# Second MoE's weights: earlier loads, decoding in 13 of 16 units, and g's low part on VectorE

## The chip, the cores and the metric

The kernel runs on one core of one Trainium2 chip. The metric is the device time of one execution in microseconds (us). A run of the profiler on that core gives the trace from which the rows below are taken. Engines are named as in the profile: PE (TensorE matmuls), PEld (its weight loads), DVE (VectorE), ACT (ScalarE), POOL (GpSimd) and SP, whose queue issues all the DMAs.

## What is computed

Three stages follow one another: a complex-decay attention (4 batches, 8 heads, 768 steps, head size 48), an MoE with a mish-like gate (384 to 2048 to 384), and a bilinear MoE (384 to 1536 to 384), on 3072 tokens.

```python
# attention: per step, S = a * S + k v^T (complex decay a, normalised), y = q . Re(S)
x = y.transpose(0, 2, 1, 3).reshape(3072, 384)
h = x @ w_in                                 # first MoE
g = h * tanh(log1p(exp(min(h, 20))))
x = g @ w_out
a, b = x @ w_a, x @ w_b                      # second MoE
out = (a * b) @ w_out2
```

All five weight matrices arrive as 64-bit floats, q, k, v and the decay as 32-bit floats.

## The kernel before

**Tiles and units.** The tokens are cut into 6 blocks of 512 (128 steps of each batch). The first MoE goes through a block in 16 units f: 9 matmuls of `moe1_h` make one 128 x 512 tile of h, `mish_factor` and `mish_product` turn it into g, and two units later (`lag`) 9 matmuls of `moe1_x2` add g times w_out into three PSUM tiles. Every product is made of three matmuls on split operands (high x high, high x low, low x high), so each weight and each activation has a high part, rounded, and a low part, the rest. `mish_product` makes them for g: `gh` on ACT in blocks 0 and 5 (`on_act`) and on DVE otherwise (L511 to L514), `gl` by one subtraction on POOL (L515). The second MoE has 12 units in each of its 6 blocks: 9 + 9 matmuls for a and b, then 12 for the output.

**Attention beside it.** The attention of block j + 1 is spread over the units of block j, in slots. Block 0 has the most beside it: the attention of block 1 and the rest of the first MoE's own weights. Block 5 has no attention left, and in its place the second MoE's weights are prepared.

**Weights.** `load_weights` handles a piece of a 64-bit matrix, 128 x 768 elements, in three steps: a DMA on SP's queue into a staging tile `wraw`; `decode`, three DVE instructions on integer words (L150 to L152) that make a 32-bit float in a tile `wf32`; and `split`, the high part on ACT and the low part on POOL (L157). `pipeline(steps, 2)` yields once a call; a call splits one piece, decodes another and starts the load of a third. The first MoE has 16 pieces, the second 18 (a, b and o for six values of j).

**Where the second MoE's pieces stand.** At the first unit of block 5 `prepare` closes the attention's pools (`att.close()`) and opens two in their place: `w2a` for the pieces of j below `EARLY` = 2, and `st2a`, with two buffers for `wf32`, for staging. The other pieces take buffers of the first MoE's weights as these are used up. Every unit of block 5 makes one call of the pipeline, and the second MoE's units make the rest. The staging pool `wst` of the first MoE's weights belongs to the attention's pools; it has two `wraw` and one `wf32`.

**Order.** Waits and order on each engine are set by the tile framework when the kernel is built: it takes the program's order as a priority and moves an instruction ahead where its model says that its inputs and buffers are there. So the order on an engine is not that of the code. Each engine goes through its own list in order: an instruction that waits holds up what stands behind it.

Of the kernel before, what the change touches and what calls it, by code (L numbers as in the profile page):

```python
# [10 lines left out]
F32 = mybir.dt.float32  # L11
F32R = mybir.dt.float32r
# [9 lines left out]
def kernel(  # L22
# [97 lines left out]
    ps_h = w1.enter_context(tc.tile_pool(name="ps_h", bufs=2, space=PSUM))  # L120
    ps_x = w1.enter_context(tc.tile_pool(name="ps_x", bufs=1, space=PSUM))

    att = right.enter_context(ExitStack())
    ap1 = att.enter_context(tc.tile_pool(name="ap1", bufs=1, side="right"))
    ap2 = att.enter_context(tc.tile_pool(name="ap2", bufs=2, side="right"))
    wst = att.enter_context(tc.tile_pool(name="wst", bufs=1, side="right"))
    am = [ap1.tile([P, HH, C], F32, name=f"am{i}") for i in range(2)]
    qT = [ap1.tile([P, HH, C], F32, name=f"qT{i}") for i in range(2)]
    W = [ap1.tile([P, H * D + PAD], F32, name=f"W{b}") for b in range(B)]
# [3 lines left out]
    def load_weights(nm, j, src, pool, place):  # L133


        a, b = src.shape[1:]
        if src.dtype == F32:
            raw = pool.tile([P, a, b], F32, tag="wraw", name="wraw", bufs=2)
            nc.sync.dma_start(out=raw, in_=src)
        else:  # L140
            b //= 2
            raw = pool.tile([P, a, b, 2], U32, tag="wraw", name="wraw", bufs=2)
            nc.sync.dma_start(out=raw.rearrange("p a b t -> p a (b t)"), in_=src)
        f = [raw]

        def decode():
            if src.dtype != F32:
                f[0] = pool.tile([P, a, b], F32, tag="wf32", name="wf32")
                fu, low, high = f[0].bitcast(U32), raw[..., 0], raw[..., 1]
                nc.vector.tensor_scalar(fu, high, 3, 0x3FFFFFFF, ALU.logical_shift_left, ALU.bitwise_and)  # L150
                nc.vector.scalar_tensor_tensor(fu, high, 0xC0000000, fu, ALU.bitwise_and, ALU.bitwise_or)  # L151
                nc.vector.scalar_tensor_tensor(fu, low, 29, fu, ALU.logical_shift_right, ALU.bitwise_or)  # L152

        def split():
            hi, lo = weights[nm, j] = [place(f"w{nm}{i}{j}", [P, a, b]) for i in "hl"]
            act(out=hi, in_=f[0], func=AF.Copy)
# [349 lines left out]
    def mish_product(p, m, on_act):  # L506

        nc.vector.scalar_tensor_tensor(m, m, 2.5, p, ALU.subtract, ALU.mult)  # L508
        gh = mp.tile([P, TN], F32R, tag="gh", name="gh")
        gl = mp.tile([P, TN], F32R, tag="gl", name="gl")  # L510
        if on_act:  # L511
            act(out=gh, in_=m, func=AF.Copy)
        else:
            nc.vector.tensor_copy(gh, m)  # L514
        nc.gpsimd.tensor_tensor(gl, m, gh.bitcast(F32), ALU.subtract)  # L515
        return gh, gl

    x2ps = {}
# [21 lines left out]

    x2h, x2l = {}, {}

    def load_w2(pool, early):


        for j in range(NF2 // 2):
            def place(name, shape, j=j):
                return early.tile(shape, F32R, name=name) if j < EARLY else shared(name, shape)

            for nm, src in (("a", wcols(w2_a, j)), ("b", wcols(w2_b, j)), ("o", wrow(w2_out, j))):  # L550
                yield lambda nm=nm, j=j, src=src, place=place: load_weights(nm, j, src, pool, place)

    def load_x2(b, pool):

        xh = x2h[b] = xp.tile([P, KM, TN], F32R, tag="xh", name="xh2")
        xl = x2l[b] = xp.tile([P, KM, TN], F32R, tag="xl", name="xl2")

        def step(t):
            raw = pool.tile([P, KM, C], F32, tag="xr", name="xr", bufs=2)
            nc.sync.dma_start(out=raw, in_=x2_d[b][:, t:t + C].rearrange("(k p) t -> p k t", p=P))  # L560

            def split():
                s = slice(t, t + C)
# [140 lines left out]
    mp = w1.enter_context(tc.tile_pool(name="mp", bufs=3))  # L704

    EARLY = 2

    def prepare():

        att.close()  # L710
        early = right.enter_context(tc.tile_pool(name="w2a", bufs=1, side="right"))
        spool = right.enter_context(tc.tile_pool(name="st2a", bufs=2, side="right"))
        steps = list(load_w2(spool, early))
        steps[3 * EARLY:3 * EARLY] = load_x2(0, spool)
        prep_pool.append(spool)
        yield from pipeline(steps, 2)

    prep_pool = []
    units = [(b, f) for b in range(NB) for f in range(NF)]
    ready, lag = {}, 2  # L720
    prep = None
    for ui in range(len(units) + lag):
        if ui < len(units):
            blk, f = units[ui]
            if f == 0:
                base = slot[0]
                want = ends[blk + 1] if blk + 1 < NB else n_slots
                if slot[0] == n_slots:
                    prep = prepare()
            p = moe1_h(blk, f, ps_a if prep and f % 2 else ps_h)  # L730
            do_w()
            run_to(base + (want - base) * (2 * f + 1) // (2 * NF))
            m = mish_factor(p)
            if prep:
                next(prep, None)
        if ui >= lag:
            moe1_x2(*units[ui - lag], *ready.pop(ui - lag))
        if ui < len(units):
            run_to(base + (want - base) * (2 * f + 2) // (2 * NF))
            ready[ui] = mish_product(p, m, blk in (0, NB - 1))  # L740

    w1.close()
    spool = prep_pool[0]
    p2 = allp.enter_context(tc.tile_pool(name="p2", bufs=3))
    one = allp.enter_context(tc.tile_pool(name="one", bufs=1))
    ps_o = allp.enter_context(tc.tile_pool(name="ps_o", bufs=1, space=PSUM))
# [208 lines left out]
```

## Time and profile before

| what | value |
|---|---|
| median of three runs (lowest to highest) | 1170.1 us (1168.77 to 1170.27) |
| the profiled execution's own time | 1166.57 us |
| its span, first to last instruction | 1164.9 us |
| PE busy | 1074.6 us (92%) |
| DVE busy | 711.3 us (61%) |
| ACT busy | 632.1 us (54%) |
| POOL busy | 350.1 us (30%) |
| granted TensorE clock, mean | 0.975 |

A row of a timeline is an instruction with its start and its duration, and in brackets how long its engine sat idle before it and what ended that. A row of windows gives, for a stretch of time, its length, how long PE, PEld, DVE, ACT and POOL were busy in it and with how many instructions, then the granted clock (1.00 is full speed), the DMA share and GB/s. DVE and POOL durations include time in which the instruction stands still for whatever reason, so the same form can have very different durations; the minimum is what it takes undisturbed.

### The profile page before, as it was taken

What the parts mean: (1) busy time and instruction counts of PE and PEld (TensorE: products, weight loads), DVE (VectorE), ACT (ScalarE), POOL (GpSimd) and SP (SyncE); (2) the same over time, 40 slices, a digit from 0 to 9 for tenths busy, and PEclk for the clock granted to TensorE, in tenths of its full rate; (3) what the DMA queues carried; (4) which work ended last, traced back from release to release, by engine and by line L of the source; (5) the groups of instructions that cost most, each with busy time, mean ns of one, the idle gap of its engine ahead of it and who ended that gap; (6) DMA issues with size and microseconds to landing.
All of it is one profiled execution on the core that took longest, in us unless ns stands there. A gap on an engine that the chain in (4) does not pass through costs nothing.

```text
span 1164.9 us, 15523 instructions
## 1 busy us (share of the span) xinstructions
PE 1074.6 (92%) x5788; PEld 904.7 (78%) x5788; DVE 711.3 (61%) x1062; ACT 632.1 (54%) x1050; POOL 350.1 (30%) x314
## 2 busy tenths in 40 slices
PE   2978887999999999999997788999999999999997
PEld 1856666888788878878875566888888888888886
DVE  5777989777777777778658998556242232322221
ACT  7767877878787877878756663212121221221221
POOL 6254665544444444444325663000000000000000
PEclk9988899999999999999998989999999999999999
DMA  7634553322233332223025444324010010100000
GB/s 132 139 104 116 136 153 66 90 49 48 56 82 68 64 75 49 48 55 82 22 82 163 138 134 148 102 87 151 1 55 1 9 47 1 34 7 1 28 1 29
DMA packets 187226, 83.01 MB, mean 71 GB/s; under 512 B 143821, under 2 KB 171530, under 8 KB 187146
## 3 DMA queue, kind: packets, MB, share of 16 engines
q1 hardware_dynamic: 187146, 81.97, 27.8%
q8 instruction: 47, 0.77, 0.3%
q14 instruction: 33, 0.27, 0.1%
HBM read 68.51 MB, written 13.43 MB: 70 GB/s over the span
## 4 chain that ended last, share of the span: by engine, by line
PE 46%; DVE 7%; ACT 2%; issue 1%; POOL 1%; DMA 1%; DVEq 0%; POOLq 0%; ACTq 0%; SPq 0%
PE ops L604 13%; PE psb L579 13%; PE psa L579 12%; PE hps L493 3%; PE x2ps L527 3%; DVE wf L151 2%; DVE wf L150 1%; ACT m L48 1%; DVE m L508 1%; DVE m L499 1%; PE py L372 1%; DVE wf L152 1%; POOL gl L515 1%; PE psc L348 1%; DMA wraw<-in_moe_w_a_dram 0%
## 5 line engine op out<-in xcount | busy, mean ns | idle before, releaser
L515 POOL TENSOR_TENSOR gl<-m,gh 128x512 fp32r<-128x512 f32 x96 | 136.3, 1419 | 130.8 <-DVE gh L514 99.4
L590 DVE TENSOR_TENSOR a_sb<-a_sb,psb 128x512 f32<-128x512 f32 x72 | 49.3, 685 | 198.2 <-PE psb L579 198.1
L48 ACT ACTIVATE m<-m 128x512 f32<-128x512 f32 x192 | 119.9, 627 | 70.8 <-DVE m L499 69.0
L48 ACT ACTIVATE ph<-a_sb 128x512 fp32r<-128x512 f32 x72 | 45.5, 632 | 179.4 <-DVE a_sb L590 179.4
L527 PE MATMUL x2ps<-gl,wouth 128*128 128x512 f32 x288 | 117.1, 407 | 20.2 <-POOL gl L515 20.2
L493 PE MATMUL hps<-xh,winh 128*128 128x512 f32 x288 | 122.5, 425 | 8.6 <-DVE xh L433 3.0
L48 ACT ACTIVATE a_sb<-psa 128x512 f32<-128x512 f32 x72 | 42.8, 596 | 159.0 <-PE psa L579 158.1
L493 PE MATMUL hps<-xl,winh 128*128 128x512 f32 x288 | 118.6, 412 | 4.6 <-DVE xl L434 4.6
L527 PE MATMUL x2ps<-gh,wouth 128*128 128x512 f32 x288 | 118.7, 416 | 2.8 <-ACT gh L48 2.8
L493 PE MATMUL hps<-xh,winl 128*128 128x512 f32 x288 | 117.4, 408 | 2.3 <-POOL winl L157 2.3
L527 PE MATMUL x2ps<-gh,woutl 128*128 128x512 f32 x288 | 115.5, 401 | 0.0
L508 DVE SCALAR_TENSOR_TENSOR m<-m,hps 128x512 f32<-128x512 f32 x96 | 65.4, 681 | 54.8 <-ACT m L48 54.7
L604 PE MATMUL ops<-woh,ph 128*128 128x384 f32 x288 | 97.2, 337 | 0.0
L604 PE MATMUL ops<-woh,pl 128*128 128x384 f32 x288 | 97.2, 337 | 0.0
L604 PE MATMUL ops<-wol,ph 128*128 128x384 f32 x288 | 96.8, 336 | 0.0
L579 PE MATMUL psb<-xh,wbh 128*128 128x512 f32 x216 | 84.7, 392 | 0.7 <-ACT a_sb L48 0.7
L579 PE MATMUL psa<-xh,wal 128*128 128x512 f32 x216 | 85.3, 395 | 0.0
L579 PE MATMUL psa<-xl,wah 128*128 128x512 f32 x216 | 85.3, 395 | 0.0
L579 PE MATMUL psa<-xh,wah 128*128 128x512 f32 x216 | 84.7, 392 | 0.0
L579 PE MATMUL psb<-xh,wbl 128*128 128x512 f32 x216 | 84.4, 391 | 0.0
L579 PE MATMUL psb<-xl,wbh 128*128 128x512 f32 x216 | 84.3, 390 | 0.0
L527 PEld LDWEIGHTS x2ps<-gl,wouth 128*128 128x128 f32 x288 | 55.7, 193 | 35.0 <-POOL gl L515 25.2
(138 smaller groups left out, 2479.6 us busy)
## 6 DMA issues: line engine op xcount, KB each, us to landing
wraw<-in_moe_w_out_dram SPq DMA_DIRECT2D x14, 768.0 KB
wraw<-in_moe_w_in_dram SPq DMA_DIRECT2D x8, 768.0 KB
re<-in_a_re_dram SPq DMA_DIRECT2D x24, 192.0 KB
im<-in_a_im_dram SPq DMA_DIRECT2D x24, 192.0 KB
q<-in_q_dram SPq DMA_DIRECT2D x24, 192.0 KB
k<-in_k_dram SPq DMA_DIRECT2D x24, 192.0 KB
v<-in_v_dram SPq DMA_DIRECT2D x24, 192.0 KB
x_d<-x2o SPq DMA_DIRECT2D x18, 256.0 KB
```

The source lines that it names most:

```text
L48: x = nc.scalar.activation(**kw)
L150: nc.vector.tensor_scalar(fu, high, 3, 0x3FFFFFFF, ALU.logical_shift_left, ALU.bitwise_and)
L151: nc.vector.scalar_tensor_tensor(fu, high, 0xC0000000, fu, ALU.bitwise_and, ALU.bitwise_or)
L152: nc.vector.scalar_tensor_tensor(fu, low, 29, fu, ALU.logical_shift_right, ALU.bitwise_or)
L348: nc.tensor.matmul(p[:, i, :], lhsT=st["kT", c, hf][:, i, :], rhs=st["qT", c, hf][:, i, :], start=True, stop=True)
L493: nc.tensor.matmul(p, lhsT=w[:, kk, :], rhs=x[:, kk, :], start=(i == 0), stop=(i == len(ops) - 1))
L508: nc.vector.scalar_tensor_tensor(m, m, 2.5, p, ALU.subtract, ALU.mult)
L515: nc.gpsimd.tensor_tensor(gl, m, gh.bitcast(F32), ALU.subtract)
L527: nc.tensor.matmul(x2ps[m], lhsT=w[:, ms], rhs=g, start=(f == 0 and i == 0), stop=(f == NF - 1 and i == 2),)
L579: nc.tensor.matmul(p, lhsT=w[:, kk, :], rhs=x[:, kk, :], start=(i == 0), stop=(i == len(ops) - 1))
L590: nc.vector.tensor_tensor(a_sb, a_sb, pb, ALU.mult)
L604: nc.tensor.matmul(ops_t[t], lhsT=x[:, tsl], rhs=w, start=(f == 0 and i == 0), stop=(f == NF2 - 1 and i == 2),)
```

## The change

Three things are changed. First, `wst` is opened ahead of the attention's pools, so that it survives `att.close()`, and the second MoE's pieces use it for staging: two `wraw`, one `wf32`. Second, the pipeline of these pieces is made once, ahead of the loop, with the four steps that read x2 of block 0 after the first three pieces; it is called in the last two units of block 4 and in the 13 units of block 5 with f % 5 != 4, and in the second MoE's units as before. Third, `gl` is made on DVE in blocks 0 and 5. The pools `w2a` and `st2a` (the latter now for x2's tiles alone) are still opened at the start of block 5.

```diff
+    wst = right.enter_context(tc.tile_pool(name="wst", bufs=1, side="right"))
     att = right.enter_context(ExitStack())
...
-    wst = att.enter_context(tc.tile_pool(name="wst", bufs=1, side="right"))
...
-        nc.gpsimd.tensor_tensor(gl, m, gh.bitcast(F32), ALU.subtract)
+        (nc.vector if on_act else nc.gpsimd).tensor_tensor(gl, m, gh.bitcast(F32), ALU.subtract)
...
-                yield lambda nm=nm, j=j, src=src, place=place: load_weights(nm, j, src, pool, place)
+                yield lambda nm=nm, j=j, src=src, place=place: load_weights(nm, j, src, wst, place)
...
-    def prepare():
+    early, spool = [], []
+
+    def make_room():
 
         att.close()
-        early = right.enter_context(tc.tile_pool(name="w2a", bufs=1, side="right"))
-        spool = right.enter_context(tc.tile_pool(name="st2a", bufs=2, side="right"))
-        steps = list(load_w2(spool, early))
-        steps[3 * EARLY:3 * EARLY] = load_x2(0, spool)
-        prep_pool.append(spool)
-        yield from pipeline(steps, 2)
+        early.append(right.enter_context(tc.tile_pool(name="w2a", bufs=1, side="right")))
+        spool.append(right.enter_context(tc.tile_pool(name="st2a", bufs=2, side="right")))
+
+    steps = list(load_w2(early))
+    steps[3:3] = load_x2(0)
+    prep = pipeline(steps, 2)
...
-                if slot[0] == n_slots:
-                    prep = prepare()
-            p = moe1_h(blk, f, ps_a if prep and f % 2 else ps_h)
+                if blk == NB - 1:
+                    make_room()
+            p = moe1_h(blk, f, ps_a if blk == NB - 1 and f % 2 else ps_h)
...
-            if prep:
+            if blk == NB - 1 and f % 5 != 4 or blk == NB - 2 and f >= NF - 2:
                 next(prep, None)
```

**SP, the loads.** Before, the first three loads of the second MoE's weights stand behind the last read of x for block 5, the first of them with the waits for the attention's pools:

```order
L427 DMA x_6027<-yt_d5_73 128x3x128
L143 DMA wraw_6093<-in_moe2_w_a_dram 128x3x512
L143 DMA wraw_6125<-in_moe2_w_b_dram 128x3x512
L560 DMA xr_6333<-x2_d0_74 128x3x128
L560 DMA xr_6373<-x2_d0_74 128x3x128
L538 DMA x2_d4_78<-x2o_6136 128x512
L143 DMA wraw_6170<-in_moe2_w_out_dram 128x2x768
```

Now the framework has brought all three far ahead, to the end of block 0, right behind the first MoE's last pieces; here are the first two, beside the attention's loads for block 2:

```order
L313 DMA g_1857<-end_d0_80 48x8x1
L143 DMA wraw_6018<-in_moe2_w_a_dram 128x3x512
L143 DMA wraw_6052<-in_moe2_w_b_dram 128x3x512
L207 DMA v_2145<-in_v_dram 128x8x48
L192 DMA q_1922<-in_q_dram 128x8x48
```

The first piece is decoded there too, among DVE's last work for block 0; its split needs the pool `w2a` and stays at the start of block 5.

**DVE, the middle of block 5.** Before, two decodes with one unit's two mish instructions (L499, L508) between them:

```order
L150 TENSOR_SCALAR wf32_6625<-wraw_6549 128x768
L151 SCALAR_TENSOR_TENSOR wf32_6625<-wraw_6549,wf32_6625 128x768
L152 SCALAR_TENSOR_TENSOR wf32_6625<-wraw_6549,wf32_6625 128x768
L499 TENSOR_SCALAR m_6437<-hps_6427 128x512
L508 SCALAR_TENSOR_TENSOR m_6399<-m_6399,hps_6389 128x512
L150 TENSOR_SCALAR wf32_6665<-wraw_6589 128x768
```

Now the same stretch has each unit's `gl` (L515) as well, at one time inside a decode and at another between two; every L150 here has a wait for POOL, on which the split of the piece before frees the only `wf32`:

```order
L150 TENSOR_SCALAR wf32_6544<-wraw_6468 128x768
L151 SCALAR_TENSOR_TENSOR wf32_6544<-wraw_6468,wf32_6544 128x768
L515 TENSOR_TENSOR gl_6341<-m_6320,gh_6340 128x512
L152 SCALAR_TENSOR_TENSOR wf32_6544<-wraw_6468,wf32_6544 128x768
L508 SCALAR_TENSOR_TENSOR m_6354<-m_6354,hps_6344 128x512
L499 TENSOR_SCALAR m_6388<-hps_6378 128x512
L515 TENSOR_TENSOR gl_6375<-m_6354,gh_6374 128x512
L150 TENSOR_SCALAR wf32_6584<-wraw_6508 128x768
```

**DVE, the end of block 5.** The instruction that takes the first MoE's last result out of PSUM is L535. Before, it stands behind L151 of the 18th and last decode:

```order
L150 TENSOR_SCALAR wf32_7092<-wraw_6994 128x768
L151 SCALAR_TENSOR_TENSOR wf32_7092<-wraw_6994,wf32_7092 128x768
L535 TENSOR_SCALAR x2o_6706<-x2ps1_6176 128x512
L564 CAST xh2_6835<-xr_6945 128x3x128
L152 SCALAR_TENSOR_TENSOR wf32_7092<-wraw_6994,wf32_7092 128x768
```

Now it stands behind L151 of the 14th, and four decodes come after it, among the second MoE's first units (L591 and L593, which were L590 and L592):

```order
L150 TENSOR_SCALAR wf32_6926<-wraw_6822 128x768
L566 TENSOR_TENSOR xl2_6825<-xr_6881,xh2_6824 128x3x128
L151 SCALAR_TENSOR_TENSOR wf32_6926<-wraw_6822,wf32_6926 128x768
L535 TENSOR_SCALAR x2o_6695<-x2ps1_6195 128x512
L152 SCALAR_TENSOR_TENSOR wf32_6926<-wraw_6822,wf32_6926 128x768
...
L150 TENSOR_SCALAR wf32_6979<-wraw_6879 128x768
L151 SCALAR_TENSOR_TENSOR wf32_6979<-wraw_6879,wf32_6979 128x768
L591 TENSOR_TENSOR a_sb_6733<-a_sb_6733,psb_6723 128x512
```

The decodes ahead of L535 in block 5 went from 18 to 13 (the second to the 14th piece).

## Rows read from the trace of the kernel before

**Rows 1.** Windows: block 0, blocks 1-4, 5, second MoE; PE PEld DVE ACT POOL busy.

```profile
76.00:219.00 143.00, 120.07 (x672) 95.76 (x673) 119.11 (x164) 109.54 (x188) 81.69 (x63) 0.89 0.44 111
219.50:601.80 382.30, 373.33 (x2342) 313.58 (x2341) 284.56 (x476) 306.05 (x509) 168.23 (x170) 1.00 0.27 59
601.80:711.30 109.50, 85.60 (x323) 64.56 (x322) 99.63 (x103) 66.97 (x103) 63.45 (x35) 0.92 0.48 152
714.90:1164.90 450.00, 443.27 (x2133) 389.98 (x2133) 152.72 (x222) 92.17 (x154) 0.52 (x1) 1.00 0.13 39
```

**Rows 2.** Chain of waits from 570 to 760 us: start us, us, what.

```profile
583.83 2.06 PE x2ps L527 x9
...
671.29 1.91 DVE wf L151
...
733.96 2.10 PE ops L604 x12
```

**Rows 3.** Groups of instructions, 601 to 712 us: xcount | busy us, mean ns | idle before.

```profile
L151 DVE SCALAR_TENSOR_TENSOR wf<-wraw,wf 128x768 uint32<-128x768 uint32 x18 | 31.2, 1732 | 0.3
L515 POOL TENSOR_TENSOR gl<-m,gh 128x512 fp32r<-128x512 f32 x18 | 30.0, 1669 | 19.3 <-DVE gh L514 10.2 <-ACT gh L48 9.1
...
L152 DVE SCALAR_TENSOR_TENSOR wf<-wraw,wf 128x768 uint32<-128x768 uint32 x18 | 20.6, 1146 | 0.2
...
L150 DVE TENSOR_SCALAR wf<-wraw 128x768 uint32<-128x768 uint32 x18 | 18.3, 1015 | 1.5 <-DMA wraw<-in_moe_w_a_dram 1.5
```

**Rows 4.** Durations of single lines, min/median/max ns: L150 in block 5, L592, L629.

```profile
L150 DVE TENSOR_SCALAR wf<-wraw x18: 544/554/2120, 607.9 to 707.6; 128x768 uint32<-128x768 uint32 x18
L592 DVE TENSOR_TENSOR pl<-a_sb,ph x72: 680/692/695, 717.1 to 1153.4; 128x512 fp32r<-128x512 f32 x72
L629 DVE TENSOR_REDUCE mins<-look x8: 1353/1353/1354, 720.3 to 807.5; 128x1 f32<-128x1152 f32 x8
```

**Rows 5.** Timeline of one decode's turn in block 5: start us, us, instruction.

```profile
667.07 0.96 DVE L152 SCALAR_TENSOR_TENSOR wf<-wraw,wf 128x768 uint32<-128x768 uint32 x1
667.94 0.68 DVE L499 TENSOR_SCALAR m<-hps 128x512 f32<-128x512 f32 x1
...
668.06 0.85 ACT L48 ACTIVATE wah<-wf 128x768 fp32r<-128x768 f32 x1 [2.24 <-DVE wf L152]
668.54 0.68 DVE L508 SCALAR_TENSOR_TENSOR m<-m,hps 128x512 f32<-128x512 f32 x1
...
668.98 1.85 POOL L157 TENSOR_TENSOR wal<-wf,wah 128x768 fp32r<-128x768 f32 x1 [2.77 <-ACT wah L48]
669.14 2.12 DVE L150 TENSOR_SCALAR wf<-wraw 128x768 uint32<-128x768 uint32 x1
...
670.84 1.53 POOL L515 TENSOR_TENSOR gl<-m,gh 128x512 fp32r<-128x512 f32 x1
671.29 1.90 DVE L151 SCALAR_TENSOR_TENSOR wf<-wraw,wf 128x768 uint32<-128x768 uint32 x1
...
673.23 0.96 DVE L152 SCALAR_TENSOR_TENSOR wf<-wraw,wf 128x768 uint32<-128x768 uint32 x1
```

**Rows 6.** Timeline of DVE: block 5's begin, second decode, last decode, L535.

```profile
601.78 1.38 DVE L434 TENSOR_TENSOR xl<-x,xh 128x384 fp32r<-128x384 f32 x1
...
613.31 1.58 DVE L150 TENSOR_SCALAR wf<-wraw 128x768 uint32<-128x768 uint32 x1
...
707.60 0.55 DVE L150 TENSOR_SCALAR wf<-wraw 128x768 uint32<-128x768 uint32 x1
...
710.56 0.69 DVE L535 TENSOR_SCALAR x2o<-x2ps 128x512 f32<-128x512 f32 x1 [0.47 <-PE x2ps L527]
```

**Rows 7.** Waits in block 0: us in total, times, longest us.

```profile
POOL gl L515 <- ACT gh L48: 15.0, 7, 4.7
```

**Rows 8.** Timeline in block 0: POOL's gl and DVE's L150 beside it.

```profile
79.74 1.29 POOL L515 TENSOR_TENSOR gl<-m,gh 128x512 fp32r<-128x512 f32 x1
79.81 1.63 DVE L150 TENSOR_SCALAR wf<-wraw 128x768 uint32<-128x768 uint32 x1 [2.22 <-POOL winl L157]
```

More of the change, by code (lines that the diff above doesn't have):

```diff
@@ L541, with load_w2, load_x2 @@
     x2h, x2l = {}, {}
-    def load_w2(pool, early):
+    def load_w2(early):
         for j in range(NF2 // 2):
             def place(name, shape, j=j):
-                return early.tile(shape, F32R, name=name) if j < EARLY else shared(name, shape)
+                return early[0].tile(shape, F32R, name=name) if j < EARLY else shared(name, shape)
             for nm, src in (("a", wcols(w2_a, j)), ("b", wcols(w2_b, j)), ("o", wrow(w2_out, j))):
-                yield lambda nm=nm, j=j, src=src, place=place: load_weights(nm, j, src, pool, place)
-    def load_x2(b, pool):
-        xh = x2h[b] = xp.tile([P, KM, TN], F32R, tag="xh", name="xh2")
-        xl = x2l[b] = xp.tile([P, KM, TN], F32R, tag="xl", name="xl2")
+                yield lambda nm=nm, j=j, src=src, place=place: load_weights(nm, j, src, wst, place)
+    def load_x2(b):
         def step(t):
-            raw = pool.tile([P, KM, C], F32, tag="xr", name="xr", bufs=2)
+            if t == 0:
+                x2h[b] = xp.tile([P, KM, TN], F32R, tag="xh", name="xh2")
+                x2l[b] = xp.tile([P, KM, TN], F32R, tag="xl", name="xl2")
+            xh, xl = x2h[b], x2l[b]
+            raw = spool[0].tile([P, KM, C], F32, tag="xr", name="xr")
             nc.sync.dma_start(out=raw, in_=x2_d[b][:, t:t + C].rearrange("(k p) t -> p k t", p=P))
@@ L706 @@
     EARLY = 2
-    def prepare():
+    early, spool = [], []
+    def make_room():
         att.close()
-        early = right.enter_context(tc.tile_pool(name="w2a", bufs=1, side="right"))
-        spool = right.enter_context(tc.tile_pool(name="st2a", bufs=2, side="right"))
-        steps = list(load_w2(spool, early))
-        steps[3 * EARLY:3 * EARLY] = load_x2(0, spool)
-        prep_pool.append(spool)
-        yield from pipeline(steps, 2)
-    prep_pool = []
+        early.append(right.enter_context(tc.tile_pool(name="w2a", bufs=1, side="right")))
[3 more added lines that the diff above has]
+    prep = pipeline(steps, 2)
     units = [(b, f) for b in range(NB) for f in range(NF)]
     ready, lag = {}, 2
-    prep = None
     for ui in range(len(units) + lag):
@@ L742 @@
     w1.close()
-    spool = prep_pool[0]
     p2 = allp.enter_context(tc.tile_pool(name="p2", bufs=3))
@@ L759 @@
                 if f == 2:
-                    xq = load_x2(b + 1, spool)
+                    xq = load_x2(b + 1)
                 for i, fn in enumerate(xq):
```

## The prediction

> **What bounds the kernel now.** I read the windows by stage first, to see which stage has time to give. The second MoE keeps PE busy for 443.3 of 450.0 us and blocks 1 to 4 for 373.3 of 382.3 [rows 1]: hardly anything is to be had there. Block 5 takes 109.5 us with PE busy for 85.6 and DVE for 99.6; block 0 takes 143.0 with 120.1 and 119.1 [rows 1]. A unit of the first MoE is two groups of nine matmuls of 2.06 us [rows 2], so block 5's 16 units need 16 x 4.12 = 65.9 us of PE: some 43 us are lost to something else. The chain of waits says what: in block 5 it runs through DVE's decodes [rows 2].
>
> Next, the groups of block 5 against undisturbed durations. L150 takes 0.55 us undisturbed [rows 4] and 1.02 in the mean; L152 takes 0.96 in a row of the timeline [rows 5], 1.15 in the mean, and L151, of the same form, 1.73 [rows 3]. Over 18 decodes DVE stands still for 18 x (0.46 + 0.77 + 0.19) = 25.6 us inside these three. One decode's turn shows why: L150 starts at 669.14, while POOL's split runs (668.98 to 670.83), and ends 0.43 us after it; L151 starts at 671.29, while POOL's gl runs (670.84 to 672.37), and ends 0.82 us after that [rows 5]. DVE's instructions on SBUF stand still beside POOL's, while L499 and L508, which read PSUM, keep their 0.68. A turn is 667.07 to 673.23 = 6.16 us; on average, second to last decode, (707.60 - 613.31) / 16 = 5.89 us [rows 6]. So **DVE, held up by POOL, bounds block 5**, at one turn for each of 18 decodes.
>
> **The change part by part.**
>
> *Loads.* Three loads move to the end of block 0. In block 5 only the first decode waited for one, 1.5 us [rows 3], so the early loads by themselves are worth little. On SP they wait for staging that is free by then, and the attention's reads behind them have a block's time. The first piece's decode moves too: 2.47 us of DVE near the end of block 0, where I cost it at nothing, and 2.5 us if nothing covers it.
>
> *Block 5, its begin.* The first split still waits for the attention's pools, that is for L434, which ends at 601.78 + 1.38 = 603.16 [rows 6]. Then ACT's high part, 0.85, POOL's low part, 1.85, and two hand-overs of 0.03 and 0.07 us [rows 5]: the second decode's L150, which waits for them with the only wf32, starts at about 606.0. Before, it started at 613.31. What is queued behind that wait on DVE are L499 and L508 of block 5's first unit and of block 4's last; PE has a unit's matmuls to go on with.
>
> *Block 5, its turns.* L535, the end of the first MoE, stands behind the 14th decode's L151 instead of the 18th's. A turn of the new order, from L150 to L150: 0.55 + 0.96 + 0.96 = 2.47 for the decode, then from L152's end to the split's end 668.03 to 670.83 = 2.80 [rows 5], with a hand-over 5.3 us. L499 and L508 (0.60 from start to start) fit into the 2.80 us. What does not fit is added by the order's count, over the twelve turns from the second L150 to the 14th:
> - twelve turns of 5.3: 63.6;
> - gl is a subtraction of two SBUF tiles, as L592, 0.69 us alone [rows 4], 0.60 where the next overlaps. Four stand right behind L152, ahead of POOL's start: free. Eight stand behind an L508, wait for gh on ACT, come when POOL has started and stand still like L150: 8 x 0.6 = 4.8. Four stand inside a decode: 2.4;
> - six L499 and six L508 inside decodes: 12 x 0.6 = 7.2;
> - four x2 splits, a cast and block 4's L535 inside decodes: about 3.0. Five x2 splits behind POOL's split, at about 0.5 each: 2.5;
> - in two turns ACT makes the high part only after the rest of a mish chain: 1.3.
>
> Sum 84.8. The 14th L150 is then at 606.0 + 84.8 = 690.8, and L535, after an x2 split and L151 (0.55 + 0.96), at 692.3 instead of 710.56: **18.3 us less**. PE is not late there: 603.2 + 65.9 = 669, and some 8 us for the last unit's way. The skipped calls (f = 4, 9, 14) and the four decodes that go to the second MoE are what makes this: a turn itself is not shorter, since it carries 16 units in 13 decodes and gl on top. From both sides: if turns stay at 5.89, 12 x 5.89 = 70.7, L150 at 676.7, L535 2.95 us behind it as before (707.60 to 710.56) at 679.7, 30.9 less; if every turn has one more wait of 1 us for ACT, 6.3 less. I take the count, because it follows the rows of one turn.
>
> *gl in block 0.* Where POOL's gl runs beside L150, L150 takes 1.63 instead of 0.55 [rows 8]: 1.08 lost, against 0.6 for gl on DVE. With 13 decodes in this block the best is 13 x 0.48 = 6 us back; with no relief it is 16 x 0.69 = 11.0 us more. DVE has idle time there (143.0 - 119.1 = 23.9 us) in which gl can lie. I take 3 us less.
>
> The Trainium skill speaks against this part: Perfetto Trace Analysis, section Optimizing Scalar/DVE Operations, has it that work of a saturated DVE may be offloaded, to GpSimd even, though the two share a port so that moving work between them might not help. Here the work goes the other way, onto the engine that bounds; by that rule alone both blocks would pay for gl, which is the second rival below. The rows of one turn speak for its second half: POOL's gl already costs DVE about as much as its own would.
>
> *Second MoE.* Four decodes of 2.47 us lie among its first five units: 9.9, and 6.9 for ten products and low parts of 0.69, five reductions of 1.35 [rows 4] 6.8, about 1 us of each split's wait uncovered, 4.0: 27.6 us of DVE. PE needs for these units 5 x 4.12 and three output groups of 2.10 [rows 2]: 26.9. POOL and ACT are nearly idle there [rows 1]. PE can be a PSUM tile ahead, so I charge 2 us, from 0 to 8.
>
> *Sum.* -18.3 - 3 + 2 = -19.3 us on the profiled execution's 1166.57 (its span is 1164.9, the rest lies around it): 1147.3. The median of the runs is 3.5 us above that execution, so the forecast is 1170.1 - 19.3 = **1150.8 us**.
>
> **The rivals.**
>
> *First: the cadence holds.* DVE, without POOL's gl, fills the gaps better than my count says, and turns stay at 5.89 us: 30.9 instead of 18.3, 1170.1 - 30.9 - 3 + 2 = 1138.2 us. For it: the framework mixes other work into the waits, as it did before. Against: one wf32 where there were two, and 1.3 units in a turn.
>
> *Second: gl costs its full price.* Block 0 pays 11.0 instead of getting 3 back: 1170.1 - 18.3 + 11.0 + 2 = 1164.8 us. For it: DVE is busy for 119.1 of 143.0 us there. Against: 1.08 us of an L150 beside one gl [rows 8].
>
> *Third, slower: DVE inherits POOL's waits for gh.* POOL waited 15.0 us for ACT's gh in block 0 [rows 7] and 9.1 in block 5 [rows 3], with nothing urgent behind. On DVE, a queue in order, L499 and L508 of the next units stand behind the same wait. If all of it is paid, with gl's 11.0 in block 0: -18.3 + 9.1 + 15.0 + 11.0 + 2 = +18.8, 1188.9 us. It decides from 16.3 us of such costs, about 1 us a unit in block 0. Against: the order puts work between most L508 and their gl, and DVE waits 2.22 us for a split at such a place anyway [rows 8].
>
> *That the change does not do what it says:* the early loads could bring nothing because the first split still waits for the attention's pools. Then the second decode starts as before, the 7.3 us of the begin are lost, and the time is 1158. This lies in the forecast's own range.
>
> **How the numbers follow.** Forecast 0.61, with its own range 1143 to 1160; first rival 0.20; second 0.12; third 0.07. The range that should hold 8 in 10 leaves out the third rival, the faster half of the first and the slowest of the second: 1137 to 1166. A measurement of this kernel can tell about 0.2% (2.3 us) from no change. Faster by more: 0.60 of the forecast, 0.20, and two thirds of the second rival, together 0.88; within: 0.05; slower: 0.07.
>
> **What would show it.** In the profile after: block 5 shorter by 10 to 30 us, the second MoE's begin earlier by as much; 13 decodes ahead of L535 in it and four behind; the wait of PE for POOL's gl gone from it; L151 near 0.96 us, L150 idle for POOL's split instead of stretched, and gl stretched where POOL's split runs beside it; a turn of 6 to 7.3 us; block 0 within 6 us of its 143. I am wrong if DVE's idle time before gl, for gh, is more than some 10 us in a block, if PE waits in the second MoE's first units for more than 8 us, or if block 5 is as long as before although it has five decodes less.

## The result, and the profile after

The changed kernel takes 1143.16 us (median of 4 runs, 1142.78 to 1143.89) against 1169.92 us (4 runs, 1168.77 to 1170.27) for the kernel before, measured beside it: a ratio of 0.9774, with a 95% interval of 0.9757 to 0.9791. The forecast was 1150.8 us, in a range of 1137 to 1166. The profiled execution of after took 1143.28 us, its span 1141.5 us.

Windows of the kernel after, over the stages of [rows 1]: block 0, blocks 1 to 4, block 5, second MoE, with the same columns.

```profile
76.00:214.90 138.90, 115.45 (x675) 91.18 (x674) 122.53 (x184) 110.57 (x188) 62.17 (x47) 0.94 0.50 134
215.50:597.50 382.00, 373.37 (x2340) 313.44 (x2341) 284.72 (x475) 306.33 (x509) 169.34 (x171) 1.00 0.28 60
597.50:686.10 88.60, 76.51 (x318) 58.21 (x317) 76.70 (x103) 63.66 (x99) 26.71 (x15) 1.00 0.42 132
690.50:1141.50 451.00, 443.27 (x2133) 389.96 (x2133) 162.46 (x234) 95.84 (x159) 7.65 (x5) 1.00 0.14 44
```

Nearly all of the gain is block 5's: 109.5 us in [rows 1] (that window reaches 0.7 us beyond the marks used below), 88.6 now. POOL is busy there for 26.7 us instead of 63.5, DVE for 76.7 instead of 99.6, and the granted clock is 1.00, 2.4 GHz throughout, where the mean of 0.92 had a part at 1.2 GHz. Block 0 gives about 4 us, and blocks 1 to 4 and the second MoE stay as they were.

In one place before's chain of waits runs through PE at the lower clock (0.50 from 621.8 to 627.8 us). Here are the matmul groups of the chain there and at the next place, at full clock (start us, us, what):

```profile
623.22 3.78 PE x2ps L527 x8
627.00 2.85 PE hps L493 x9
...
643.26 2.11 PE x2ps L527 x8
645.37 2.07 PE hps L493 x9
```

So some 2.5 us of what block 5 gained can be the clock; no run tests that by itself.

Groups of DVE in block 5 of after (count, busy us and mean ns, idle time before and what ended it), to be read against [rows 3]:

```profile
L515 DVE TENSOR_TENSOR gl<-m,gh 128x512 fp32r<-128x512 f32 x16 | 18.3, 1145 | 3.2 <-ACT gh L48 3.2
L151 DVE SCALAR_TENSOR_TENSOR wf<-wraw,wf 128x768 uint32<-128x768 uint32 x13 | 12.4, 953 | 0.2
...
L152 DVE SCALAR_TENSOR_TENSOR wf<-wraw,wf 128x768 uint32<-128x768 uint32 x12 | 11.4, 952 | 0.1
...
L150 DVE TENSOR_SCALAR wf<-wraw 128x768 uint32<-128x768 uint32 x13 | 7.2, 552 | 6.6 <-POOL wal L157 3.6 <-POOL wol L157 2.9
```

The three instructions of a decode now take what they take undisturbed: L151 0.953 us instead of 1.732, L150 0.552 instead of 1.015. What is left of the standing still is in gl, 1.145 us, and in L150's idle time before it, 6.6 us.

Timeline of DVE in after, at the begin and the end of block 5, to be read against [rows 6]:

```profile
597.46 1.38 DVE L434 TENSOR_TENSOR xl<-x,xh 128x384 fp32r<-128x384 f32 x1
601.73 0.56 DVE L150 TENSOR_SCALAR wf<-wraw 128x768 uint32<-128x768 uint32 x1 [2.89 <-POOL wal L157]
...
684.29 0.55 DVE L150 TENSOR_SCALAR wf<-wraw 128x768 uint32<-128x768 uint32 x1
...
686.10 0.68 DVE L535 TENSOR_SCALAR x2o<-x2ps 128x512 f32<-128x512 f32 x1
```

From L434 to the last L535 block 5 now takes 686.10 - 597.46 = 88.6 us; in [rows 6] it was 710.56 - 601.78 = 108.8. These two instructions are the marks of block 5 in the table below, and block 0 ends with the first x2o of ACT. "Other" is what DVE was not busy in block 5. Decodes are the L150 in block 5 that stand ahead of the last L535.

| kernel | median us | end of block 0 | block 5 | DVE busy in it | other | POOL busy in it | decodes | second MoE |
|---|---|---|---|---|---|---|---|---|
| before | 1169.9 | 218.4 | 108.8 | 98.9 | 9.9 | 62.7 | 18 | 454.3 |
| after | 1143.2 | 214.9 | 88.6 | 76.7 | 11.9 | 26.8 | 13 | 455.4 |
| gl back on POOL | 1170.0 | 222.1 | 107.7 | 83.4 | 24.3 | 54.5 | 15 | 454.9 |
| before, gl on DVE | 1150.5 | 213.3 | 91.1 | 87.8 | 3.3 | 29.4 | 15 | 460.1 |
| gl on DVE in block 5 alone | 1150.3 | 221.1 | 88.6 | 76.8 | 11.9 | 26.7 | 13 | 454.8 |
| calls in all 16 units | 1142.7 | 213.9 | 88.6 | 76.6 | 12.0 | 26.8 | 13 | 454.6 |
| one more subtraction on POOL | 1171.9 | 227.4 | 102.3 | 90.0 | 12.4 | 53.8 | 13 | 457.5 |
| one more copy on POOL | 1153.2 | 219.0 | 92.8 | 79.9 | 13.0 | 39.5 | 13 | 457.9 |
| second MoE's low parts on DVE | 1129.6 | 215.1 | 75.0 | 70.4 | 4.6 | 2.8 | 10 | 455.0 |
| two wf32 | 1134.8 | 209.9 | 88.1 | 85.1 | 3.0 | 35.7 | 15 | 453.7 |
| before, low parts on DVE | 1145.5 | 218.7 | 85.9 | 81.0 | 4.9 | 28.8 | 14 | 455.9 |
| low parts on DVE, two wf32 | 1126.2 | 208.4 | 75.7 | 72.0 | 3.7 | 2.8 | 12 | 456.7 |
| all low parts on DVE | 1123.4 | 208.4 | 75.6 | 70.4 | 5.2 | 2.8 | 10 | 455.4 |
| all low parts on DVE, two wf32 | 1122.3 | 202.9 | 75.3 | 72.1 | 3.2 | 2.8 | 12 | 456.5 |

The kernel before had medians of 1167.7, 1168.1 and 1169.0 us beside the experiments; the ratios below are to these. Moving an instruction to another engine also changes the order that the framework builds, and with it the number of decodes ahead of the last L535.

### The profile page after: what moved, and what is told of

It is laid out like the page before. It is cut to its first block, busy times and chain, and to the rows that moved or that the text cites. A ratio compares the mean times of both kernels' runs of the same rounds, so it can differ in the third digit from the quotient of the medians.

```text
span 1141.5 us, 15490 instructions
## 1 busy us (share of the span) xinstructions
PE 1063.2 (93%) x5788; PEld 895.6 (78%) x5788; DVE 700.8 (61%) x1094; ACT 632.2 (55%) x1050; POOL 302.5 (26%) x282
## 4 chain that ended last, share of the span: by engine, by line
PE 46%; DVE 4%; issue 3%; ACT 2%; POOL 2%; DMA 1%; SPq 0%; POOLq 0%; DVEq 0%; ACTq 0%
PE ops L605 13%; PE psb L580 13%; PE psa L580 13%; PE hps L493 3%; PE x2ps L527 3%; ACT m L48 2%; PE py L372 1%; DMA x_d<-x2o 1%; POOL wal L157 1%; PE psc L348 1%; DVE m L499 1%; POOL wol L157 0%; POOL wbl L157 0%; DVE m L508 0%; DVE gl L515 0%
## 5 line engine op out<-in xcount | busy, mean ns | idle before, releaser
L591 DVE TENSOR_TENSOR a_sb<-a_sb,psb 128x512 f32<-128x512 f32 x72 | 49.4, 686 | 193.2 <-PE psb L580 193.0
L527 PE MATMUL x2ps<-gl,wouth 128*128 128x512 f32 x288 | 114.6, 398 | 9.0 <-DVE gl L515 7.6
L493 PE MATMUL hps<-xl,winh 128*128 128x512 f32 x288 | 116.2, 403 | 4.3 <-DVE xl L434 4.3
L527 PE MATMUL x2ps<-gh,wouth 128*128 128x512 f32 x288 | 116.3, 409 | 2.2 <-ACT gh L48 2.2
L515 POOL TENSOR_TENSOR gl<-m,gh 128x512 fp32r<-128x512 f32 x64 | 88.1, 1376 | 103.0 <-DVE gh L514 95.7
L508 DVE SCALAR_TENSOR_TENSOR m<-m,hps 128x512 f32<-128x512 f32 x96 | 65.4, 682 | 53.9 <-ACT m L48 53.8
L580 PE MATMUL psa<-xh,wal 128*128 128x512 f32 x216 | 85.1, 394 | 0.0
L493 PEld LDWEIGHTS hps<-xh,winh 128*128 128x128 f32 x288 | 55.6, 193 | 26.8 <-DVE m L508 7.6
```

What stands on the lines that cost most here:

```text
L493: nc.tensor.matmul(p, lhsT=w[:, kk, :], rhs=x[:, kk, :], start=(i == 0), stop=(i == len(ops) - 1))
L515: (nc.vector if on_act else nc.gpsimd).tensor_tensor(gl, m, gh.bitcast(F32), ALU.subtract)
L527: nc.tensor.matmul(x2ps[m], lhsT=w[:, ms], rhs=g, start=(f == 0 and i == 0), stop=(f == NF - 1 and i == 2),)
L580: nc.tensor.matmul(p, lhsT=w[:, kk, :], rhs=x[:, kk, :], start=(i == 0), stop=(i == len(ops) - 1))
L591: nc.vector.tensor_tensor(a_sb, a_sb, pb, ALU.mult)
```

## The experiments

### Which part of the change makes it

The change with gl left on POOL:

```diff
-        (nc.vector if on_act else nc.gpsimd).tensor_tensor(gl, m, gh.bitcast(F32), ALU.subtract)
+        nc.gpsimd.tensor_tensor(gl, m, gh.bitcast(F32), ALU.subtract)
```

> The changed kernel with gl back on POOL in blocks 0 and 5; all else as changed. My theory (the decodes that leave block 5 and its earlier begin make the gain; gl is a small part of it, some 4 us in block 0 and about 0.5 us in each of block 5's twelve turns): 1143.2 + 4 + 6 = about 1153 us, block 0 back to about its old length. Rival (POOL's gl was what held DVE up, and taking it away is most of the gain): 1160 to 1168 us.

1169.95 us (10 runs), ratio 1.0016 (1.0006 to 1.0025), above both expectations: with gl on POOL, early loads, shared staging and later decodes together gain nothing. Block 5 of this kernel in the windows, with two of its groups:

```profile
606.40:714.10 107.70, 83.14 (x314) 62.55 (x313) 83.36 (x98) 66.88 (x102) 54.50 (x34) 0.92 0.42 132
```

```profile
L150 DVE TENSOR_SCALAR wf<-wraw 128x768 uint32<-128x768 uint32 x15 | 19.6, 1306 | 20.1 <-POOL wal L157 8.7 <-POOL wbl L157 6.5 <-POOL wol L157 4.9
L152 DVE SCALAR_TENSOR_TENSOR wf<-wraw,wf 128x768 uint32<-128x768 uint32 x15 | 15.3, 1020 | 0.4
```

Three decodes fewer than before and less standing still inside them make DVE's busy time 15.5 us shorter (98.9 to 83.4). But with a single wf32 each L150 waits for POOL's split: 20.1 us of idle time, where [rows 3] have 1.5. The one takes what the other gives.

The kernel before with gl on DVE in blocks 0 and 5, and nothing else:

```diff
-        nc.gpsimd.tensor_tensor(gl, m, gh.bitcast(F32), ALU.subtract)
+        (nc.vector if on_act else nc.gpsimd).tensor_tensor(gl, m, gh.bitcast(F32), ALU.subtract)
```

> The kernel before with gl on DVE in blocks 0 and 5 and nothing else. My theory: block 0 about 4 us shorter, block 5 still bound by 18 turns and at most 4 us shorter, 1162 to 1166 us. Rival (gl is most of the gain): 1146 to 1155 us. Slower rival (DVE inherits the waits for gh): above 1172 us.

1150.52 us, ratio 0.9853 (0.9837 to 0.987): the rival held. This one line takes block 5 from 108.8 to 91.1 us, and the framework's order for it has 15 decodes ahead of L535 instead of 18. Its groups of DVE there:

```profile
L150 DVE TENSOR_SCALAR wf<-wraw 128x768 uint32<-128x768 uint32 x15 | 17.7, 1179 | 1.4 <-DMA wraw<-in_moe_w_a_dram 1.4
L151 DVE SCALAR_TENSOR_TENSOR wf<-wraw,wf 128x768 uint32<-128x768 uint32 x15 | 17.6, 1176 | 0.1
L152 DVE SCALAR_TENSOR_TENSOR wf<-wraw,wf 128x768 uint32<-128x768 uint32 x15 | 14.7, 981 | 0.1
L515 DVE TENSOR_TENSOR gl<-m,gh 128x512 fp32r<-128x512 f32 x16 | 14.5, 908 | 0.0
```

DVE got 14.5 us of gl and was busy for 11.1 us less. In the decodes' three lines, against 0.55, 0.96 and 0.96 undisturbed, the standing still fell from 25.6 us over 18 decodes to 15 x (0.63 + 0.22 + 0.02) = 13.1 us. The three decodes that left are 3 x 2.47 = 7.4 us of DVE, so this kernel doesn't give gl's price alone. But the kernel of the run before this has 15 decodes there too, with gl on POOL and one wf32, and its block 5 is 107.7 us. What the rest of the change adds on top is in this kernel's difference from after: 2.5 us of block 5, and 4.7 us in the second MoE, which is longer here than in any other kernel; of that, one wait of PE for ACT's a, 4.5 us against 1.3 in after, is what the trace names.

The change with gl on DVE in block 5 alone:

```diff
-        (nc.vector if on_act else nc.gpsimd).tensor_tensor(gl, m, gh.bitcast(F32), ALU.subtract)
+        (nc.vector if low_dve else nc.gpsimd).tensor_tensor(gl, m, gh.bitcast(F32), ALU.subtract)
...
-            ready[ui] = mish_product(p, m, blk in (0, NB - 1))
+            ready[ui] = mish_product(p, m, blk in (0, NB - 1), blk == NB - 1)
```

> The changed kernel with gl on DVE in block 5 alone, on POOL in block 0. My theory: block 0 gives its 4 us back, 1147 us. Rival (block 0 gets nothing from gl; what it won comes from the other order): 1143 us, as the changed kernel.

1150.27 us, ratio 0.9853 (0.9831 to 0.9876), above both expectations. Block 5 is the same to 0.1 us, and block 0 ends 6.2 us later (221.1 against 214.9): that is what gl on DVE is worth in block 0.

Calls in all 16 units of block 5:

```diff
-            if blk == NB - 1 and f % 5 != 4 or blk == NB - 2 and f >= NF - 2:
+            if blk == NB - 1 or blk == NB - 2 and f >= NF - 2:
```

> The changed kernel with the preparation called in all 16 units of block 5 instead of 13. My theory: three more decodes stand ahead of the first MoE's end, each 2.5 us of DVE and about 1 us of waiting, and the second MoE gets 1 us back: about 1152 us, block 5 some 10 us longer. Rival (the number of decodes in block 5 does not matter, the framework moves them as it likes): 1143 us.

1142.67 us, ratio 0.9787 (0.9771 to 0.9804): after's time, as the rival had it. The instructions on every engine stand in after's order, and 13 decodes lie ahead of L535 as in after. Which unit makes the call decides nothing here. My reading, which no run shows, is that the framework moves a decode to where its buffers are free, and with one wf32 that is once per split.

### Why gl on POOL is so expensive

Two theories were left. Either POOL's subtraction costs by running, as DVE stands still beside it; or it costs by its place in POOL's list, where PE waits for it behind the weights' low parts. The longest waits of PE's matmuls in block 5, of before and of after (us in total, times, longest):

```profile
PE x2ps L527 <- POOL gl L515: 20.2, 12, 3.7
```

```profile
PE x2ps L527 <- DVE gl L515: 7.6, 9, 1.4
```

These alone fit both. So the next kernel is after, with gl on DVE, and in blocks 0 and 5 one more subtraction on POOL per unit, whose result nobody reads:

```diff
+        if on_act:
+            spare = mp.tile([P, TN], F32, tag="spare", name="spare", bufs=1)
+            nc.gpsimd.tensor_tensor(spare, m, gh.bitcast(F32), ALU.subtract)
```

> The kernel after, with gl where it is (DVE), and one more subtraction of the same two tiles and size on POOL per unit of blocks 0 and 5, into a tile that nobody reads or waits for (extra work; the output is unchanged). POOL's list in block 5 then reads as in the kernel before, a subtraction between two low parts of weights, but nothing on PE's way waits for it. Theory P, POOL's subtraction costs by running, since DVE's instructions on SBUF stand still beside it: block 5 goes from 88.6 us back to 100 to 108, block 0 grows by 3 to 6, the whole 1157 to 1168 us; L151 in block 5 back from 0.95 us in the mean to 1.3 or more. Theory Q, what cost time was gl's place in POOL's queue, PE waiting for it behind the weights' low parts: block 5 stays at 88 to 91, the whole 1143 to 1147, and L151 may be stretched without anything being late for it.

1171.94 us, ratio 1.0029 (1.0017 to 1.004). In block 5 the first theory held, and the whole is longer than either theory had it: work that nothing waits for undoes the whole gain. No wait in blocks 0 and 5 of this trace names the added subtraction, and DVE's order in block 5 is after's, instruction for instruction. Its block 0 and block 5 in the windows, and groups of DVE and POOL from 600 to 720 us (one decode of the second MoE is among them):

```profile
76.00:227.40 151.40, 119.49 (x673) 93.80 (x674) 139.50 (x183) 110.32 (x187) 86.98 (x62) 0.90 0.46 120
610.30:712.70 102.40, 83.61 (x323) 61.99 (x322) 90.02 (x103) 64.38 (x100) 53.78 (x31) 0.95 0.36 114
```

```profile
L515 DVE TENSOR_TENSOR gl<-m,gh 128x512 fp32r<-128x512 f32 x16 | 22.6, 1414 | 3.4 <-ACT gh L48 3.4
L150 DVE TENSOR_SCALAR wf<-wraw 128x768 uint32<-128x768 uint32 x14 | 15.4, 1098 | 7.6 <-POOL wol L157 4.2 <-POOL wal L157 3.4
L151 DVE SCALAR_TENSOR_TENSOR wf<-wraw,wf 128x768 uint32<-128x768 uint32 x14 | 14.9, 1068 | 0.2
...
L508 DVE SCALAR_TENSOR_TENSOR m<-m,hps 128x512 f32<-128x512 f32 x19 | 12.9, 679 | 5.9 <-ACT m L48 5.9
...
L518 POOL TENSOR_TENSOR spare<-m,gh 128x512 f32<-128x512 f32 x16 | 26.8, 1675 | 21.4 <-ACT gh L48 21.2
```

With the same 13 decodes and the same instructions on DVE, block 5 is 13.7 us longer, and DVE's busy time is 13.3 us longer: the time went into standing still, 0.83 us for each subtraction on POOL. L508, which reads PSUM, keeps its 0.68. I had expected it in L151 (1.3 us or more); it is 1.07, and L150 (0.55 to 1.10) and gl (1.15 to 1.41) carry most. Block 0 grew by 12.5 us, where I had expected 3 to 6: DVE is busy there for 139.5 us instead of 122.5, in an order that differs from after's in a few places of the block's last third.

The second theory is not dead altogether. With gl on POOL block 5 is 19.1 us longer than after's (107.7 and 88.6), and the unread subtractions account for 13.7 of them. The remaining 5.4 us, with 15 decodes instead of 13 and 21.1 us of PE's waits for POOL's gl, were not taken apart.

One place where DVE stands still, in the timeline of the kernel with the unread subtraction:

```profile
639.52 1.29 POOL L518 TENSOR_TENSOR spare<-m,gh 128x512 f32<-128x512 f32 x1
639.60 1.63 DVE L150 TENSOR_SCALAR wf<-wraw 128x768 uint32<-128x768 uint32 x1 [0.53 <-POOL wal L157]
```

POOL starts 0.08 us ahead and ends at 640.81; L150 ends 0.42 us after that, a little less than the 0.55 us that it takes alone. It did next to nothing beside POOL. The Trainium skill (SBUF — State Buffer, section SBUF: two separate sides) has a rule of this kind, for DVE instructions in a mode that uses two ports or with two inputs in SBUF: whichever of DVE and GpSimd starts first gets the port pair that they share for its whole instruction, and the other waits. This place agrees; L150 has one input, and no run shows its mode.

Not every DVE instruction on SBUF is held up. A cast of x for the second MoE (L568) runs within the added subtraction in its usual 0.55 us, and L151 behind it ends late, 0.82 us after POOL:

```profile
702.57 1.61 POOL L518 TENSOR_TENSOR spare<-m,gh 128x512 f32<-128x512 f32 x1
702.96 0.55 DVE L568 CAST xh<-xr 128x384 fp32r<-128x384 f32 x1
703.42 1.58 DVE L151 SCALAR_TENSOR_TENSOR wf<-wraw,wf 128x768 uint32<-128x768 uint32 x1
```

The same with a copy of m, one input, in place of the subtraction:

```diff
-            nc.gpsimd.tensor_tensor(spare, m, gh.bitcast(F32), ALU.subtract)
+            nc.gpsimd.tensor_copy(spare, m)
```

> The kernel after, with one copy of m, 128 x 512, on POOL per unit of blocks 0 and 5, into a tile that nobody reads (extra work): one input where the run before this has two. If DVE stands still beside any instruction of POOL on SBUF: block 5 is 94 us or longer, in proportion to the copy's duration, the whole 1150 us or more, and L151 longer than 1.2 us in the mean. If only POOL's instructions with two inputs do it: within 3 us of 1143, L151 at 0.95. By theory Q of the run before: within 3 us too.

1153.22 us, ratio 0.9869 (0.985 to 0.9887): the whole is where the first theory had it, but block 5 (92.8 us) and L151 (0.95 us) are not. DVE's order is after's, and block 5 is 4.2 us longer than after's. The copies and L150 in its groups:

```profile
L518 POOL COPY spare<-m 128x512 f32<-128x512 f32 x16 | 12.7, 797 | 39.4 <-DVE m L508 39.4
```

```profile
L150 DVE TENSOR_SCALAR wf<-wraw 128x768 uint32<-128x768 uint32 x14 | 9.2, 660 | 8.1 <-POOL wal L157 5.2 <-POOL wol L157 2.9
```

An instruction with one input costs too, 4.2 us of block 5 for 12.7 us of POOL, a third; for the subtractions it was 13.7 for 26.8, a half.

### Taking the rest off POOL

What is left on POOL in block 5 are the weights' low parts. The next kernel is after with those of the second MoE on DVE:

```diff
-            nc.gpsimd.tensor_tensor(lo, f[0], hi.bitcast(F32), ALU.subtract)
+            (nc.gpsimd if nm in ("in", "out") else nc.vector).tensor_tensor(lo, f[0], hi.bitcast(F32), ALU.subtract)
```

> The kernel after, with the low part of the second MoE's weights (L157) on DVE instead of POOL, so that POOL does next to nothing in block 5. Theory P: DVE gets 12 more low parts of 0.9 to 1.0 us in block 5, about 12 us, and loses what stands still there, 16 x 0.45 = 7 us of gl, 6.6 us of waits of L150 for POOL and some 1 us elsewhere: about even, block 5 86 to 91, the whole 1140 to 1148; gl's mean falls from 1.15 to 0.65 to 0.70 us. Rival, DVE's busy time alone bounds block 5 and stretching is free (it fills waits): block 5 +12, 100 or more, the whole 1154 or more.

1129.58 us, ratio 0.9667 (0.9651 to 0.9683). I had expected an even exchange in block 5 and was wrong by 11 us or more. Block 5, and gl in it:

```profile
597.70:672.70 75.00, 73.38 (x318) 58.51 (x317) 70.43 (x105) 62.22 (x97) 2.78 (x2) 1.00 0.40 125
```

```profile
L515 DVE TENSOR_TENSOR gl<-m,gh 128x512 fp32r<-128x512 f32 x16 | 11.0, 685 | 1.1 <-ACT gh L48 0.9
```

Now PE is busy for 73.4 of 75.0 us and bounds this block. My count left 13 decodes in block 5, but the framework's order for this kernel has only 10 ahead of the last L535. That is 3 x 2.47 = 7.4 us of DVE less, and the three lie in the second MoE, which is no longer for it (455.0 us). A unit goes by in 75.0 / 16 = 4.7 us, 5.5 in after, while a decode's turn, with its low part, is not shorter (7.33 us, 6.88 in after). What the three decodes are worth was not run by itself; with 12 of them in block 5 (low parts on DVE and two wf32, below) it takes 75.7 us.

After with two wf32 buffers:

```diff
-                f[0] = pool.tile([P, a, b], F32, tag="wf32", name="wf32")
+                f[0] = pool.tile([P, a, b], F32, tag="wf32", name="wf32", bufs=2)
```

> The kernel after with two wf32 buffers where it has one. Theory P: the waits of L150 for the split, 6.6 us in block 5, turn into L150s and L151s that stand still beside POOL; block 5 within 4 us of 88.6, the whole 1139 to 1146. Rival, the single buffer is what keeps block 5 from PE's pace (76.5 us of PE busy): block 5 80 to 84, the whole 1133 to 1138.

1134.77 us, ratio 0.9709 (0.9693 to 0.9726). In block 5 the first theory held, 88.1 us. L150 waits less there, and L150, L151 (1.15 us) and L152 are stretched again (590 to 690 us, with one decode of the second MoE):

```profile
L152 DVE SCALAR_TENSOR_TENSOR wf<-wraw,wf 128x768 uint32<-128x768 uint32 x16 | 19.5, 1219 | 0.0
...
L150 DVE TENSOR_SCALAR wf<-wraw 128x768 uint32<-128x768 uint32 x16 | 13.2, 831 | 2.9 <-POOL wal L157 2.9
```

The whole lies in the rival's range, but not by the rival's reason: block 0, where the first MoE's pieces use the same buffer, ends 5 us earlier (209.9).

The kernel before with the second MoE's low parts on DVE and gl left on POOL (the edit of L157 above, made in before):

> The kernel before with one change of another place: the low part of the second MoE's 18 weight pieces (L157) on DVE instead of POOL, and gl left on POOL. If DVE pays for POOL's instructions one for one (DVE's own low part, 18 x 0.95 = 17 us, against what stands still beside POOL's, some 13 us): block 5 105 to 112 us where it was 108.8, the whole 1165 to 1174. If either of the two loads on POOL by itself is cheap and only both together cost: block 5 about 91 as with gl alone off POOL, the whole 1148 to 1154.

1145.47 us, ratio 0.9803 (0.9785 to 0.9821). Both expectations were too high: block 5 is 85.9 us. Its groups of L151 and gl:

```profile
L151 DVE SCALAR_TENSOR_TENSOR wf<-wraw,wf 128x768 uint32<-128x768 uint32 x14 | 18.3, 1310 | 0.1
```

```profile
L515 POOL TENSOR_TENSOR gl<-m,gh 128x512 fp32r<-128x512 f32 x18 | 29.1, 1621 | 62.1 <-ACT gh L48 42.9 <-DVE gh L514 10.2 <-issue 6.1
```

Taking either load off POOL shortens block 5 by about 20 us (gl 17.7, low parts 22.9), and both together, with the rest of the change, by 33.8, where PE's own work ends it. So it is not gl in itself. With less of POOL's work block 5 is shorter, though not strictly (85.9 us here with POOL busy for 28.8, 88.6 in after with 26.8). These kernels have 15, 14 and 10 decodes ahead of L535 instead of 18, so only the unread subtraction and the copy, with DVE's order unchanged, give a price of POOL's work alone.

Three combinations followed. First the second MoE's low parts on DVE and two wf32, the edits of L157 and of the buffers together:

> The kernel after with the second MoE's low parts on DVE and two wf32 buffers, the two changes that gave 1129.6 and 1134.8 us alone. If the buffer's gain lies in block 0 (138.9 to 133.9 us) it adds up: 1121 to 1126. If it was the same time, block 5's, that both gave: 1128 to 1131.

1126.19 us (1124.23 to 1129.29), ratio 0.9646 (0.962 to 0.9672). It lies between the two expectations: 17.0 us below after, where the changes gave 13.6 and 8.4 us alone. What adds up is block 0's, which ends at 208.4; block 5 is no shorter (75.7 us).

Then all low parts, the first MoE's too, on DVE, and the same with two wf32:

```diff
-            nc.gpsimd.tensor_tensor(lo, f[0], hi.bitcast(F32), ALU.subtract)
+            nc.vector.tensor_tensor(lo, f[0], hi.bitcast(F32), ALU.subtract)
```

> The kernel after with the low part of all weight pieces, the first MoE's too, on DVE. Block 5 as in the run with the second MoE's alone, 75 us. Block 0 has 13 decodes, whose low part takes DVE 13 x 0.95 = 12 us there, and DVE is busy for 122.5 of its 139 us; it gets back L150's wait for POOL (6.5 us) and what stands still (L150 0.70 instead of 0.55, gl 0.85 instead of 0.69: 4.7 us). By these rows about even: block 0 136 to 141, the whole 1127 to 1132. If it goes as in block 5, where the count by busy time was too small by 14 us: block 0 125 to 131, the whole 1115 to 1121. If DVE is full: block 0 145 or more, 1136 or more.

> The run before this with two wf32 buffers as well. With no low part on POOL the buffer is free sooner, so that a second one is worth less than the 5 us that it gave block 0 before: within 3 us of the run before this. If it still gives 5 us, 5 less.

1123.35 us (1119.81 to 1125.87), ratio 0.961 (0.9582 to 0.9639), and 1122.32 us (1121.32 to 1123.63), ratio 0.9605 (0.9586 to 0.9625). These two can't be told apart. Block 0 of the one and of the other, and blocks 1 to 4 of the second, in the windows:

```profile
76.00:208.40 132.40, 115.96 (x674) 90.83 (x675) 123.00 (x201) 109.29 (x185) 32.97 (x32) 0.95 0.54 137
```

```profile
76.00:202.90 126.90, 113.92 (x671) 91.11 (x671) 122.74 (x195) 106.89 (x183) 36.99 (x32) 0.95 0.53 138
```

```profile
202.90:589.00 386.10, 376.35 (x2347) 315.44 (x2345) 285.96 (x477) 307.13 (x510) 169.82 (x171) 0.99 0.28 61
```

In block 0 too DVE takes over the low parts without being busier (123.0 us, and 122.5 in after), while POOL falls from 62.2 to 33.0. The first lies between its two expectations, 6.5 us below after's block 0. The second buffer gives 5.5 us more there, which blocks 1 to 4 give back in part (386.1 us against 382.4 in the kernel without it); why these are longer was not tried. Both are about 1.8% below the changed kernel, 4% below the kernel before.

## Why the prediction was right, and where its reason was wrong

**The number.** The spans differ by 23.4 us: block 5 -20.1 (forecast -18.3), block 0 -3.6 (-3), the second MoE +1.1 (+2), and blocks 1 to 4 -0.7 (nothing). That is 4.1 us more than the forecast's 19.3. The other 3.5 us of the 7.6 us by which it missed are an offset: I added the distance of one profiled execution of before to its median, and after's profiled execution lies at its median (1143.28 and 1143.16).

**Block 5, its begin and its turns: right.** The second decode's L150 starts 2.89 us after L434's end; 2.84 was forecast. The twelve turns take 684.29 - 601.73 = 82.6 us, forecast 84.8, and L535 follows 1.8 us later, forecast 1.5. The rows above show what the text said they would: L151 at 0.95, L150 idle for the split, gl stretched, 13 decodes ahead of L535. One place in after's timeline:

```profile
642.63 1.86 POOL L157 TENSOR_TENSOR wal<-wf,wah 128x768 fp32r<-128x768 f32 x1 [4.01 <-ACT wah L48]
...
643.11 1.93 DVE L515 TENSOR_TENSOR gl<-m,gh 128x512 fp32r<-128x512 f32 x1 [0.23 <-ACT gh L48]
...
644.97 0.55 DVE L150 TENSOR_SCALAR wf<-wraw 128x768 uint32<-128x768 uint32 x1
```

gl waits out POOL's split (to 644.49) and so delays the next decode, as counted.

**What makes it: wrong.** The step that failed is the sentence that the skipped calls and the four decodes that go to the second MoE make the gain, while a turn is not shorter. A turn is indeed not shorter (6.88 us). But the skipped calls do nothing (1142.67 us without them). Three decodes fewer ahead of L535, with gl on POOL and one wf32, gain 1.1 us there; gl off POOL gains 17.7 us by itself, also with three decodes fewer. The order has 13 decodes there only with gl on DVE: a kernel with 13 and gl on POOL was not run, so what the last two are worth stays open. The gain was in the sum all the same, in its bare turn of 5.3 us, which has every decode at its undisturbed time; I never worked out what the same order would cost with gl still on POOL, so that the number came out right beside a wrong reason. Beneath it lies a size: I had POOL's gl costing DVE "about as much as its own would". On DVE undisturbed it is 0.69 us; on POOL a subtraction of this size costs DVE 0.83 us of standing still, and besides that there is idle time, 9.9 us in block 5 of before against 3.3 with gl moved alone. The sentence that DVE's instructions on SBUF stand still beside POOL's is too broad: the cast of x does not.

**The early loads** are worth little, as said: with gl on POOL the whole is at 1.0016 of before. Of the 43 us of block 5 that I called lost to something else, some 9 are not to be had: where PE bounds the block it takes 75.0 us, not 65.9.

**Block 0: the sum right by two errors.** gl on DVE gains 6.2 us there (after against gl on DVE in block 5 alone), at the favourable bound of 6, where I took 3. The rest of the change costs 1.5 us there (against before with gl on DVE) to 3.7 us (with gl on POOL), where I took nothing for the moved decode of 2.47 us. Whether that decode is all of it was not tried.

**PE's wait for POOL's gl** was to be gone. One of 1.4 us is left, for a gl of block 4; beside it PE waits 7.6 us for DVE's gl, where it waited 20.2 us for POOL's.

**The rivals.** Turns did not hold 5.89 us: 6.88. With two wf32 buffers they do (5.80 us from the second decode on in before with gl on DVE, 5.31 in after with two wf32), but with 15 decodes ahead of L535 instead of 13, and block 5 is 91.1 and 88.1 us against after's 88.6. gl at its full price is refuted by block 0, which gains 6.2 us by it, and DVE inheriting POOL's waits for gh by its idle time before gl: 3.2 us in block 5 and 0.8 in block 0. The rule of the Trainium skill (Perfetto Trace Analysis, section Optimizing Scalar/DVE Operations) that work of a saturated DVE may go to GpSimd goes against these runs: the same work the other way gained 1.5% (gl) and 2.0% (low parts). Its second half, that moving work between these two might not help, is nearer to them: what POOL ran took DVE's time.

## What to carry to other kernels

Where DVE bounds a stage and POOL works on SBUF beside it, POOL's work isn't free: in the table block 5 is longer by 0.4 to 0.6 us for each us that POOL is busy in it, from 75 us with POOL nearly at rest, though the kernels differ in their decodes too. With DVE's order unchanged it is 0.5 for added subtractions and 0.3 for added copies. Look for DVE instructions of one form whose minimum and mean differ, see what POOL runs then, and try the work on DVE, even if DVE is the busiest engine. When a change has several parts, cost each part with the others absent; a sum can be right while the reason beside it is not.

## What was not expected of the hardware

Subtractions on POOL that nothing waits for cost most of what those cost that PE waits for: 16 of them 13.7 us of block 5, against 19.1 us for gl on POOL. A copy with one input (0.80 us on POOL) cost a third of its own time. And work moved onto the busiest engine made it less busy: DVE's busy time in block 5 fell by 11.1 us when it took over 14.5 us of gl, and in after by 6.3 us (76.7 to 70.4) when it took over 11 low parts of 0.95 us. Each time three decodes (7.4 us) left the stretch as well; without that it would be 3.7 us less, and 1.1 us more for 10.4 us of work.
